# Retention tiles 16 to 35 in pairs: one order of TensorE's products for two tiles

## The chip, the cores and the metric

One core of a Trainium2 chip. The metric is the time of one execution on the device in microseconds (us). A kernel is run several times and the median stands for it.

## The reference

Two parts. Retention: for 8 batches and 8 heads, 576 positions of 64 features. Then a mixture of experts in which each of the 4,608 tokens goes to one of 8 experts.

```python
scores = scale * np.matmul(q, k.transpose(0, 1, 3, 2))
ret = scores * np.where(rel >= 0, gamma[:, None, None] ** rel, 0.0)
x = np.matmul(ret, v)                       # then (4608, 512)
logits = x @ w_gate                         # (4608, 8), the expert is argmax
gate_w = softmax(logits)[expert]; eom = sigmoid(x @ w_output_gate)
out[token] = gate_w * eom * (relu(x[token] @ w1[expert]) @ w2[expert])
```

## The kernel before

Everything is in float32. The 4,608 rows are 36 tiles of 128 tokens; nine tiles are two batches (576 + 576 rows), so in what follows c = g % 9 is the place of tile g in its pair of batches, and tile c = 4 holds the end of one batch and the start of the next. Causality over earlier tiles is carried by a running state, the sum of k times v per head: it is kept in PSUM (`st_ps`), copied to SBUF after each tile (`stT`), and started anew at c = 0 and c = 4. The decay is folded into q and v beforehand.

The order is written out by hand: every engine, and every DMA queue, runs its instructions in the order in which the code emits them, and waits on what it needs at the head of its queue. Lines 979 to 1053 are the loop over the tiles. For tile g, TensorE gets, in this order:

- `scores(g + 1)` (L767): 32 products in an array shape of 64 x 64, into two banks of PSUM of a ring of three; VectorE then multiplies both banks by the causal mask into `S_sb` (L771, two instructions);
- the state product of tile g (L800): 16 products, 64 x 64, into `o_ps`; none at c = 0;
- scores by v (L804): 16 products, 128 x 64, onto the same `o_ps`; ScalarE copies the result to `xT` (L807), VectorE turns it to rows `xq` (L812), and SyncE stores them in DRAM (L816);
- `update(g)` (L785): 16 products, 128 x 64, into `st_ps`, copied by ScalarE to `stT` (L788); none at c = 8;
- `k_rows(g + 1)` (L745): four transposes of k, 128 x 128, into the bank `kt`, copied by ScalarE to `kn` (L750, L752), which the next update reads; none for c = 8;
- once in four tiles, `logits` (L822): 32 products, 128 x 32, and two tiles later `ranks` (L860 to L867), six products of 128 x 128 in bfloat16, which read what VectorE has made of the logits (`gate_a`, eight instructions from L828 to L849). `gate_b`, `gate_d` and `gate_c` (L872 to L902, VectorE) and two exponentials (L854, L893, ScalarE) make from these the slots and weights that GpSimd scatters to the lists of the experts.

Beside these stand, in the queues of the other engines: GpSimd multiplies q by its decay (`prep_q`, L723), four tiles ahead. From tile 23 on, ScalarE multiplies all eight heads of v by theirs (`prep_va`, L739, eight instructions a tile, three tiles ahead; five heads for tiles 20 to 22, the others go to GpSimd at L730). SyncE loads q, k and v of tile g + 6 (L690) into the buffers that tile g gives up, each load behind the last product that reads that buffer. `PLAN` (L50) says after which tiles GpSimd sends a scatter to the lists (L906, "s") or gathers rows for the first expert (L257, "g"). The weights of the first expert are rounded on ScalarE (L231) and their rests taken on VectorE (L234, two halves, one behind a tile). Behind tile 35 the products of the first expert begin (L469, `mm1_columns`).

Of the kernel before, what the change touches and what calls it, by code (L numbers as in the profile page):

```python
# [10 lines left out]
F32 = mybir.dt.float32  # L11
F32R = mybir.dt.float32r
# [37 lines left out]
PLAN = {8: "ss", 12: "ss", 16: "ss", 20: "ss", 11: "", 15: "", 19: "", 22: "sg", 23: "g", 24: "gs", 25: "gs", 26: "s",  # L50
        27: "ss", 28: "ss", 29: "sg", 30: "gg", 31: "gs", 32: "gs", 33: "gg", 34: "gs", 35: "ss"}
LISTS = (20, 28, 31)
W1_AT = (4, 11, 17, 25)


@with_exitstack
def tile_retention_moe(
# [628 lines left out]
    st_ps, stcur = [None], [None]  # L686
# [54 lines left out]
    def k_rows(g):  # L741

        kt = ps_1.tile([P, 512], F32, name="kt")
        for p in range(NP):
            T.transpose(kt[:, P * p:P * p + P], pk[g, 1][:, P * p:P * p + P], ident)  # L745
# [8 lines left out]
    def scores(g):  # L754


        sc = [banks[(2 * g + r) % 3] for r in range(2)]
        S_sb = wk.tile([P, 2, NP, P], F32, name="S_sb")
        edge = g % CPB == 4
        for pp in (0, 2):  # L760
            for late in range(2):
                for p in (pp, pp + 1):
                    h = (late + p) % 2
                    i = slice(64, P) if late else slice(0, 64) if edge else slice(0, P)
                    for r in range(2):
                        s = slice(64 * r, 64 * r + 64)
                        T.matmul(sc[r][64 * h:64 * h + 64, p, i], lhsT=pk[g, 1][s, P * p + 64 * h:P * p + 64 * h + 64],  # L767
                                 rhs=qs[g][s, p, i], start=True, stop=True, skip_group_check=True)
        m = cmat_sb[:, 1 if edge else 0].rearrange("p (a b) i -> p a b i", a=1).broadcast_to([P, 2, 2, P])
        for r in range(2):  # L770
            V.tensor_tensor(out=S_sb[:, r].rearrange("p (a b) i -> p a b i", a=2),  # L771
                            in0=sc[r].rearrange("p (a b) i -> p a b i", a=2), in1=m, op=ALU.mult)
        return S_sb

    def update(g):
        c = g % CPB
        marks["u"] = marks["v"]
        if c == 8:
            return
        if c in (0, 4):  # L780
# [8 lines left out]
        stcur[0] = stT[g % 2]  # L789

    def out_x(g, S_sb, state):
        c = g % CPB
        o = o_ps[:, :, 256 * (g % 2):256 * (g % 2) + 256]
        part = lambda p, r: o[64 * ((p + r) % 2):64 * ((p + r) % 2) + 64, r, P * (p // 2):P * (p // 2) + P]
        order = [(p, (p + i) % 2) for p in range(NP) for i in range(2)]
        if state is not None:
            w = 64 if c == 4 else P
            for p, r in order:
                s = slice(64 * r, 64 * r + 64)
                marks["q"] = T.matmul(part(p, r)[:, 0:w], lhsT=state[s, p, :], rhs=qs[g][s, p, 0:w],  # L800
                                      start=(p < 2), stop=False, skip_group_check=True).ins
        marks.setdefault("q", last[0])
        for p, r in order:
            marks["v"] = T.matmul(part(p, r), lhsT=vs[g][:, 2 * p + r, :], rhs=S_sb[:, r, p, :],  # L804
                                  start=(state is None and p < 2), stop=True, skip_group_check=True).ins
        xT[g] = wk.tile([P, KB, P], F32, name="xT", bufs=5)
        A.copy(out=xT[g].rearrange("p (r s) i -> p r s i", r=2),  # L807
               in_=o[:, :, :].rearrange("p r (s i) -> p r s i", s=2))

    def x_rows(g):  # L810
        xq = xr[g] = wk.tile([P, 4, P], F32, name="xq", bufs=3)
# [3 lines left out]
    def store_x(g):  # L815
        SP.dma_start(out=xs[4 * P * g:4 * P * (g + 1)].rearrange("(p b) c -> p b c", b=4), in_=xr[g])  # L816
# [75 lines left out]
    def exp_b(n):  # L892
        A.activation(out=gt["zs"], in_=gt["zs"], func=AF.Exp, scale=-1.0)  # L893
# [82 lines left out]
        elif what == "s":  # L976
            todo.pop(0)(by=by)

    for g in range(NTILE):
        S_sb = S_next  # L980
        prev = stcur[0] if g % CPB != 0 else None
        n, late = divmod(g - GT, GT)
        if g == 0:
            for i in range(3):
                load(5, i)
        if g > 0:
            store_x(g - 1)
        if g < 4:
            load_rest(g)
        if g == 5:  # L990
            SP.dma_start(out=ents, in_=tokid)
        if g in W1_AT:
            wl.append(load_w(1, 0, W1_AT.index(g)))
        elif 30 <= g <= 32:
            wl.append(load_w(2, 0, g - 30))
        if g in LISTS:
            load_idx(0, LISTS.index(g), LISTS.index(g) + 1)
        if g == 4:
            V.tensor_copy(base2, base)
        if 0 < g < NTILE - 1:  # L1000
# [5 lines left out]
        while min(ready) < min(g + lead + 1, NTILE):  # L1006
# [6 lines left out]
        if g + 3 < NTILE:  # L1013
            prep_va(g + 3)
        if g in (8, 16, 20, 28):
            split_w(*wl.pop(0))
        elif n >= 0 and late == 1:
            gate_a(n)
        if sub:
            sub.pop()()  # L1020
        out_x(g, S_sb, prev)
        if g == NTILE - 1:
            last_x = transp_a(2)
# [9 lines left out]
        if g + 6 < NTILE:  # L1033
            for i, m in enumerate("qvu"):
                load(g + 6, i, marks[m])
        if g == 0:
            S_next = scores(1)
        if g < 2:
            more_gq(3 + g)
        if g + 1 < NTILE and (g + 1) % CPB != CPB - 1:  # L1040
            k_rows(g + 1)
        if g in (28, 32):
            sub.append(transp_a(g // 32))
        if n >= 0 and late == 0:
            gt["ps"] = ps_1.tile([P, 512], F32, name="lg_ps")
            logits(n, gt["ps"])
        elif n >= 0 and late == 2:
            exp_b(n)
            gate_d(n)
            if n >= 5:  # L1050
                gate_c(n)
        elif 0 <= n < 5 and late == 3:
            gate_c(n)
    last_x()
    psctx.close()
    pools["ps_h"] = mctx.enter_context(tc.tile_pool(name="ps_h", bufs=2, space=PSUM, side="right", reuse_waits="tile"))
# [536 lines left out]
```

## Time and profile before

| | |
|---|---|
| median of 3 runs | 544.37 us (543.6 to 544.88) |
| the profiled execution | 543.63 us |
| its span | 541.8 us |
| TensorE busy | 524.0 us (97%) |
| VectorE, ScalarE, GpSimd busy | 412.6, 296.1, 336.7 us |
| DMA | 102.98 MB, 190 GB/s mean over the span |

The span is the time between the first and the last instruction that the profiler recorded; the execution's own time is 1.8 us longer. Busy shares are averages over the retention (about the first 140 us) and the experts (the rest), in which different things wait. A matmul's end is modelled, so consecutive matmuls overlap in the rows; the distance from one start to the next is what one of them takes of TensorE. PE is TensorE, PEld its weight loads, DVE VectorE, ACT ScalarE, POOL GpSimd, SP SyncE; L767 is line 767 of the kernel before.

### The profile page before, as it was taken

What the parts mean: (1) busy time and instruction counts of PE and PEld (TensorE: products, weight loads), DVE (VectorE), ACT (ScalarE), POOL (GpSimd) and SP (SyncE); (2) the same over time, 40 slices, a digit from 0 to 9 for tenths busy, and PEclk for the clock granted to TensorE, in tenths of its full rate; (3) what the DMA queues carried; (4) which work ended last, traced back from release to release, by engine and by line L of the source; (5) the groups of instructions that cost most, each with busy time, mean ns of one, the idle gap of its engine ahead of it and who ended that gap; (6) DMA issues with size and microseconds to landing.
All of it is one profiled execution on the core that took longest, in us unless ns stands there. A gap on an engine that the chain in (4) does not pass through costs nothing.

```text
span 541.8 us, 14890 instructions
## 1 busy us (share of the span) xinstructions
PE 524.0 (97%) x5707; PEld 479.1 (88%) x5707; DVE 412.6 (76%) x772; ACT 296.1 (55%) x566; POOL 336.7 (62%) x354
## 2 busy tenths in 40 slices
PE   7999999999999999999999999999999999999994
PEld 4887888878897988998999999899999989999982
DVE  4678688987873759997798689869958976996650
ACT  5535579888343527645744664476355447635710
POOL 2859986887787777876655476456737555101821
PEclk9999999999999999999999999999999999999998
DMA  8999899879224424636643762565276356516511
GB/s 264 365 364 378 302 332 317 302 259 318 84 67 133 139 73 159 213 122 163 220 142 103 243 225 62 169 228 187 77 225 219 103 155 225 171 39 201 172 46 36
DMA packets 60444, 102.98 MB, mean 190 GB/s; under 512 B 11492, under 2 KB 23269, under 8 KB 60372
## 3 DMA queue, kind: packets, MB, share of 16 engines
q1 hardware_dynamic: 50628, 81.65, 45.7%
q0 software_dynamic: 9312, 19.71, 11.9%
q8 instruction: 45, 0.74, 0.5%
q10 hardware_dynamic: 432, 0.66, 0.4%
q14 instruction: 27, 0.22, 0.1%
HBM read 78.26 MB, written 23.86 MB: 188 GB/s over the span
## 4 chain that ended last, share of the span: by engine, by line
PE 50%; issue 16%; DVE 11%; DMA 8%; POOL 7%; ACT 5%; SPq 1%; POOLq 0%; DVEq 0%; ACTq 0%
PE h_ps L528 6%; PE o_ps L804 5%; PE y_ps L578 5%; POOL x_q L257 5%; PE sc L767 4%; PE y_ps L609 4%; PE y_ps L528 3%; PE h_ps L578 3%; DMA out_dram<-y,idx 3%; DMA st<-in_w_dram 3%; PE h_ps L609 3%; PE o_ps L800 2%; PE y_ps L450 2%; PE kt L745 2%; PE h_ps L389 2%
## 5 line engine op out<-in xcount | busy, mean ns | idle before, releaser
L257 POOL DMA_INDIRECT x_q<-xs,gidx x139 | 162.0, 1166 | 60.6 <-issue 35.4
L543 POOL DMA_INDIRECT out_dram<-y,idx x13 | 15.2, 1170 | 67.2 <-ACT y L588 62.3
L771 DVE TENSOR_TENSOR S_sb<-sc,cmat_sb 128x512 f32<-128x512 f32 x72 | 45.7, 676 | 8.2 <-PE sc L767 8.1
L578 PE MATMUL y_ps<-w2l,hh 128*128 128x512 f32 (+1 forms) x128 | 49.9, 390 | 0.0
L578 PE MATMUL y_ps<-w2h,hh 128*128 128x512 f32 (+1 forms) x128 | 49.9, 390 | 0.0
L723 POOL TENSOR_TENSOR q<-q,gq_sb 128x512 f32<-128x512 f32 x33 | 42.3, 1283 | 10.2 <-DMA q<-in_pack_dram 6.5
L212 DVE TENSOR_TENSOR w<-st,w 128x1024 fp32r<-128x1024 f32 x21 | 25.6, 1221 | 27.6 <-ACT w L202 27.6
L906 POOL DMA_INDIRECT lst<-ents,sli x36 | 38.7, 1074 | 10.2 <-issue 5.0
L578 PE MATMUL y_ps<-w2h,hl 128*128 128x512 f32 (+1 forms) x128 | 43.6, 390 | 0.0
L528 PE MATMUL h_ps<-t,w 128*128 128x300 f32 (+4 forms) x288 | 40.7, 293 | 0.0
L804 PE MATMUL o_ps<-S_sb,v 128*64 128x128 f32 x576 | 40.0, 279 | 0.4 <-POOL v L730 0.3
L181 DVE TENSOR_TENSOR st<-st 128x512 f32<-128x512 f32 x56 | 37.2, 685 | 3.7 <-DMA st<-in_w_dram 3.0
L219 ACT CAST w2h<-st 128x1024 fp32r<-128x1024 f32 x28 | 29.3, 1046 | 18.8 <-DMA st<-in_w_dram 18.8
L543 POOL DMA_INDIRECT out_dram<-yr,idx x21 | 21.1, 1005 | 29.2 <-ACT yr L641 11.9
L528 PEld LDWEIGHTS h_ps<-t,w 128*128 128x128 f32 x288 | 38.7, 188 | 0.2 <-DVE p L511 0.2
L807 ACT COPY xT<-o_ps 128x512 f32<-128x512 f32 x36 | 21.0, 582 | 31.0 <-PE o_ps L804 30.6
L804 PEld LDWEIGHTS o_ps<-S_sb,v 128*64 128x64 f32 x576 | 31.0, 136 | 6.2 <-issue 3.4
L767 PEld LDWEIGHTS sc<-q,k 64*64 64x64 f32 x1152 | 27.5, 133 | 9.9 <-issue 6.6
L812 DVE STREAM_TRANSPOSE xq<-xT 128x512 f32<-128x512 f32 x36 | 25.4, 706 | 14.2 <-ACT xT L807 11.7
L767 PE MATMUL sc<-q,k 64*64 64x64 f32 (+1 forms) x1152 | 33.9, 248 | 2.1 <-DVE S_sb L771 1.0
L739 ACT ACTIVATE v<-v,gkf 128x64 f32<-128x64 f32 x137 | 35.0, 340 | 0.0
L223 DVE TENSOR_TENSOR w2l<-st,w2h 128x1024 fp32r<-128x1024 f32 x28 | 34.1, 1217 | 0.3
(247 smaller groups left out, 1466.2 us busy)
## 6 DMA issues: line engine op xcount, KB each, us to landing
st<-in_w_dram SPq DMA_DIRECT2D x36, 512.0 KB
st<-in_w_dram SPq DMA_DIRECT2D x56, 256.0 KB
k<-in_pack_dram SPq DMA_DIRECT2D x36, 256.0 KB
xs<-xq SPq DMA_DIRECT2D x36, 256.0 KB
q<-in_pack_dram SPq DMA_DIRECT2D x35, 256.0 KB
v<-in_pack_dram SPq DMA_DIRECT2D x35, 256.0 KB
yr<-yg SPq DMA_DIRECT2D x12, 256.0 KB
x_q<-xs,gidx POOLq DMA_INDIRECT x139
```

The lines of the kernel that those rows point to most:

```text
L181: V.tensor_tensor(out=RAW[e, q, name], in0=RAW[e, q, a], in1=RAW[e, q, b], op=op)
L257: i = G.indirect_dma_start(out=XG[e, t][:, u, :], out_offset=None, in_=seen, in_offset=bass.IndirectOffsetOnAxis(ap=gidx[:, e, 4 * t + u:4 ...
L528: last[0] = T.matmul(ps[:, b], lhsT=x[:, k, P * b:P * b + P], rhs=y[:, k], start=(j < 2 and i == 0), stop=(i == 5), skip_group_check=True).ins
L543: i = G.indirect_dma_start(out=out, out_offset=bass.IndirectOffsetOnAxis(ap=rows, axis=0), in_=y, in_offset=None, bounds_check=NT - 1, oob ...
L578: last[0] = T.matmul(ps, lhsT=a, rhs=b, start=(j == 0), stop=(j == 3 * FB - 1)).ins
L609: last[0] = T.matmul(ps[:, 0:n], lhsT=a, rhs=b, start=(j == 0), stop=(j == 3 * FB - 1)).ins
L723: (V if g < 3 else G).tensor_tensor(out=qs[g], in0=qs[g], in1=gq_sb[:, :, c0:c0 + P], op=ALU.mult)
L739: A.activation(out=v[:, h], in_=v[:, h], func=AF.Copy, scale=gk_sb[:, g % CPB, h])
L767: T.matmul(sc[r][64 * h:64 * h + 64, p, i], lhsT=pk[g, 1][s, P * p + 64 * h:P * p + 64 * h + 64], rhs=qs[g][s, p, i], start=True, stop=Tru ...
L771: V.tensor_tensor(out=S_sb[:, r].rearrange("p (a b) i -> p a b i", a=2), in0=sc[r].rearrange("p (a b) i -> p a b i", a=2), in1=m, op=ALU.mult)
L804: marks["v"] = T.matmul(part(p, r), lhsT=vs[g][:, 2 * p + r, :], rhs=S_sb[:, r, p, :], start=(state is None and p < 2), stop=True, skip_gr ...
L906: i = G.indirect_dma_start(out=lst, out_offset=bass.IndirectOffsetOnAxis(ap=sli[:, t, :], axis=0), in_=ent[:, t], in_offset=None)
```

## The change

The loop over the tiles ends at tile 15. `out_x` is taken apart into `q_state`, `s_v` and `x_copy`, `k_rows` and `scores` are told which banks to use, and a new loop takes two tiles a step. Four banks (the ring of three and `kt`) are used as two sets of two. The masked scores of every third tile go into memory of a later buffer (`hl2`), so that three of them can live at once. q is prepared three tiles ahead, v on ScalarE up to tile a + 2 and then b + 2.

```diff
+SOLO = 16
...
-    for g in range(NTILE):
+    for g in range(SOLO):
...
+    S, ready_va = {SOLO: S_next}, [SOLO + 3]
+    quads = [*banks, ps_1.tile([P, 512], F32, name="kt").rearrange("p (a b) -> p a b", a=NP)]
+    quad_of = lambda a, i: quads[2 * ((a // 2 + i) % 2):2 * ((a // 2 + i) % 2) + 2]
...
+    store_x(SOLO - 1)
+    ahead(SOLO)
+    split_w(*wl.pop(0))
+    update(SOLO)
+    indirect("s", marks["u"])
+    more(SOLO + 6, 1, "u")
+    rows_of((SOLO + 1, SOLO + 2), quads[2:4])
+    indirect("s", marks["t"])
+    lows.pop(0)()
+    count(SOLO // GT - 1)
+
+    for a in range(SOLO + 1, NTILE, 2):
+        o, b = a - 1, a + 1
+        n, odd = divmod(a - GT - 1, GT)
+        on = b < NTILE
+        pa, pb = (PLAN.get(g, "s") + ".." for g in (a, b))
+        if a > SOLO + 1:
+            store_x(o - 2)
+            store_x(o - 1)
+        weights(a)
+        ahead(a)
+        if not odd:
+            gate_a(n)
+        S[a] = scores(a, quad_of(a, 0))
+        if not odd:
+            exp_a(n)
+        indirect(pa[0], marks["s"])
+        more(a + 6, 1, "s")
+        fresh = True
+        for g in (o, a):
+            if g % CPB:
+                q_state(g, states[g - 1], fresh)
+                fresh = False
+            more(g + 6, 0, "q")
+        if on:
+            weights(b)
+            ahead(b)
+            S[b] = scores(b, quad_of(a, 1))
+            more(b + 6, 1, "s")
+        indirect(pa[1], marks["s"])
+        if not odd:
+            ranks(n)
+            gate_b(n)
+            gate_d(n)
+        elif sub:
+            sub.pop()()
+        if on:
+            update(a)
+        if not odd:
+            exp_b(n)
+            gate_c(n)
+        for g in (o, a):
+            s_v(g, S.pop(g), False)
+            more(g + 6, 2, "v")
+            if g == o:
+                indirect(pb[0] if on else ".", marks["v"])
+        for g in (o, a):
+            x_copy(g)
+        if b in (20, 28):
+            split_w(*wl.pop(0))
+        if on:
+            update(b)
+            indirect(pb[1], marks["u"])
+        if odd:
+            for i in range(2):
+                if lows:
+                    lows.pop(0)()
+        if not on:
+            last_x = transp_a(2)
+        for g in (o, a):
+            x_rows(g)
+        rows_of((a + 2, b + 2), quad_of(a, 0))
+        if a in (27, 31):
+            sub.append(transp_a(a // 31))
+        if odd and on:
+            count(n + 1)
```

`ahead(g)` is `prep_q` up to tile g + 3, `prep_v` and `prep_va` up to g + 2; `weights(g)` loads weights and lists at the tiles where they were loaded before; `more(g, i, m)` loads q, k or v (i = 0, 1, 2) of tile g behind the products marked m; `rows_of` is `k_rows` for the tiles that need it; `count(n)` is `logits(n)`.

## Rows read from the trace of the kernel before

**Rows 1.** A stretch of four tiles: us, then busy PE, PEld, DVE, ACT, POOL, clock, DMA, GB/s.

```profile
86.25:100.99 14.74, 14.40 (x376) 12.54 (x375) 12.69 (x32) 14.22 (x51) 13.33 (x16) 1.00 0.97 314
```

**Rows 2.** Timeline of PE, one tile: start us, us, what.

```profile
65.73 0.90 PE L767 MATMUL sc<-q,k 64*64 64x128 f32 x32
66.45 0.62 PE L800 MATMUL o_ps<-q,stT 64*64 64x128 f32 x16
67.00 1.09 PE L804 MATMUL o_ps<-S_sb,v 128*64 128x128 f32 x16
67.92 0.63 PE L785 MATMUL st_ps<-v,kn 128*64 128x64 f32 x16
68.49 0.66 PE L745 MATMUL kt<-ident,k 128*128 128x128 f32 x4
69.07 0.90 PE L767 MATMUL sc<-q,k 64*64 64x128 f32 x32
```

**Rows 3.** Timeline of PE, windows of some 0.05 us across two changes of shape.

```profile
66.78 0.29 PE L800 MATMUL o_ps<-q,stT 64*64 64x128 f32 x4
67.00 0.33 PE L804 MATMUL o_ps<-S_sb,v 128*64 128x128 f32 x2
...
68.27 0.29 PE L785 MATMUL st_ps<-v,kn 128*64 128x64 f32 x4
68.49 0.33 PE L745 MATMUL kt<-ident,k 128*128 128x128 f32 x1
```

**Rows 4.** Timeline of PEld, the same tile; idle time before a group in brackets.

```profile
65.73 0.76 PEld L767 LDWEIGHTS sc<-q,k 64*64 64x64 f32 x32 [0.17 <-issue]
66.39 0.43 PEld L800 LDWEIGHTS o_ps<-q,stT 64*64 64x64 f32 x16
67.00 0.85 PEld L804 LDWEIGHTS o_ps<-S_sb,v 128*64 128x64 f32 x16 [0.17 <-issue]
```

**Rows 5.** Timeline of PE, tiles 24 to 30: idle before a group in brackets.

```profile
100.99 1.08 PE L822 MATMUL lg_ps<-xT,wg_sb 128*32 128x128 f32 x32 [0.34 <-DVE zs L900]
...
111.84 1.01 PE L767 MATMUL sc<-q,k 64*64 64x128 f32 x30 [0.27 <-DVE S_sb L771]
...
121.28 0.67 PE L800 MATMUL o_ps<-q,stT 64*64 64x128 f32 x16 [0.34 <-ACT stT L788]
```

**Rows 6.** Timeline of ACT: one tile of eight heads, a weight's rounding, an exponential.

```profile
97.02 0.56 ACT L807 COPY xT<-o_ps 128x512 f32<-128x512 f32 x1
97.48 0.37 ACT L788 COPY stT<-st_ps 128x256 f32<-128x256 f32 x1
97.75 0.58 ACT L752 COPY kn<-kt 128x512 f32<-128x512 f32 x1
98.23 2.03 ACT L739 ACTIVATE v<-v,gkf 128x64 f32<-128x64 f32 x8
...
114.45 1.04 ACT L231 CAST w<-st 128x1024 fp32r<-128x1024 f32 x1
...
139.98 0.20 ACT L893 ACTIVATE zs<-zs 128x4 f32<-128x4 f32 x1 [1.18 <-DVE zs L874]
```

**Rows 7.** Timeline of DVE: gate_a from first to last of eight, masks, a weight's rest.

```profile
89.42 0.32 DVE L828 STREAM_TRANSPOSE lg_ps<-lg_ps 128x128 f32<-128x128 f32 x1
...
91.14 0.23 DVE L849 TENSOR_REDUCE oh<-oh 128x8 bf16<-128x40 bf16 x1
...
95.84 1.28 DVE L771 TENSOR_TENSOR S_sb<-sc,cmat_sb 128x512 f32<-128x512 f32 x2
...
98.25 2.18 DVE L234 TENSOR_TENSOR w<-st,w 128x512 fp32r<-128x512 f32 x1
```

**Rows 8.** Timelines of SP and POOL: loads of tile 22, and the wait for its q.

```profile
74.27 0.33 SPq L690 DMA_DIRECT2D q<-in_pack_dram  x1
...
75.66 0.39 SPq L690 DMA_DIRECT2D v<-in_pack_dram  x1
...
80.46 1.27 POOL L723 TENSOR_TENSOR q<-q,gq_sb 128x512 f32<-128x512 f32 x1 [0.85 <-DMA q<-in_pack_dram]
```

More of the change, by code (lines that the diff above doesn't have):

```diff
@@ L739, in prep_va, with k_rows @@
             A.activation(out=v[:, h], in_=v[:, h], func=AF.Copy, scale=gk_sb[:, g % CPB, h])
-    def k_rows(g):
-        kt = ps_1.tile([P, 512], F32, name="kt")
+    def k_rows(g, kt=None):
+        if kt is None:
+            kt = ps_1.tile([P, 512], F32, name="kt")
         for p in range(NP):
-            T.transpose(kt[:, P * p:P * p + P], pk[g, 1][:, P * p:P * p + P], ident)
+            marks["t"] = T.transpose(kt[:, P * p:P * p + P], pk[g, 1][:, P * p:P * p + P], ident).ins
         kn[g] = wk.tile([P, 512], F32, name="kn")
@@ L752, in k_rows, with scores @@
             A.copy(out=kn[g], in_=kt)
-    def scores(g):
-        sc = [banks[(2 * g + r) % 3] for r in range(2)]
-        S_sb = wk.tile([P, 2, NP, P], F32, name="S_sb")
+    def scores(g, sc=None):
+        sc = sc or [banks[(2 * g + r) % 3] for r in range(2)]
+        if g > SOLO and g % 3 == 0:
+            S_sb = hpa.tile([P, 2, CW], F32R, name="hl2").bitcast(F32).rearrange("p a n -> p (a n)")[:, 0:8 * P]
+            S_sb = S_sb.rearrange("p (r a i) -> p r a i", r=2, a=NP)
+        else:
+            S_sb = wk.tile([P, 2, NP, P], F32, name="S_sb")
         edge = g % CPB == 4
@@ L766, in scores @@
                         s = slice(64 * r, 64 * r + 64)
-                        T.matmul(sc[r][64 * h:64 * h + 64, p, i], lhsT=pk[g, 1][s, P * p + 64 * h:P * p + 64 * h + 64],
-                                 rhs=qs[g][s, p, i], start=True, stop=True, skip_group_check=True)
+                        marks["s"] = T.matmul(sc[r][64 * h:64 * h + 64, p, i],
+                                              lhsT=pk[g, 1][s, P * p + 64 * h:P * p + 64 * h + 64],
+                                              rhs=qs[g][s, p, i], start=True, stop=True, skip_group_check=True).ins
         m = cmat_sb[:, 1 if edge else 0].rearrange("p (a b) i -> p a b i", a=1).broadcast_to([P, 2, 2, P])
@@ L788, in update, with q_state, s_v, x_copy @@
         A.copy(out=stT[g % 2], in_=st_ps[0])
[L789 to L805, printed above, removed]
+        stcur[0] = states[g] = stT[g % 2]
+    o_of = lambda g: o_ps[:, :, 256 * (g % 2):256 * (g % 2) + 256]
+    part = lambda g, p, r: o_of(g)[64 * ((p + r) % 2):64 * ((p + r) % 2) + 64, r, P * (p // 2):P * (p // 2) + P]
+    both = [(p, (p + i) % 2) for p in range(NP) for i in range(2)]
+    def q_state(g, state, fresh=True):
+        w = 64 if g % CPB == 4 else P
+        for p, r in both:
+            s = slice(64 * r, 64 * r + 64)
+            marks["q"] = T.matmul(part(g, p, r)[:, 0:w], lhsT=state[s, p, :], rhs=qs[g][s, p, 0:w],
+                                  start=(fresh and p < 2), stop=False, skip_group_check=True).ins
+    def s_v(g, S_sb, fresh):
+        for p, r in both:
+            marks["v"] = T.matmul(part(g, p, r), lhsT=vs[g][:, 2 * p + r, :], rhs=S_sb[:, r, p, :],
+                                  start=(fresh and p < 2), stop=True, skip_group_check=True).ins
+    def x_copy(g):
         xT[g] = wk.tile([P, KB, P], F32, name="xT", bufs=5)
         A.copy(out=xT[g].rearrange("p (r s) i -> p r s i", r=2),
-               in_=o[:, :, :].rearrange("p r (s i) -> p r s i", s=2))
+               in_=o_of(g).rearrange("p r (s i) -> p r s i", s=2))
+    def out_x(g, S_sb, state):
+        if state is not None:
+            q_state(g, state)
+        marks.setdefault("q", last[0])
+        s_v(g, S_sb, state is None)
+        x_copy(g)
     def x_rows(g):
@@ L1005, in tile_retention_moe @@
         plan = PLAN.get(g, "s" if g > 8 else "") + ".."
-        while min(ready) < min(g + lead + 1, NTILE):
+        while min(ready) < g + lead + 1:
             if ready[0] <= ready[1]:
@@ L1032, in tile_retention_moe @@
         indirect(plan[1], marks["u"])
-        if g + 6 < NTILE:
-            for i, m in enumerate("qvu"):
-                load(g + 6, i, marks[m])
+        for i, m in enumerate("qvu"):
+            load(g + 6, i, marks[m])
         if g == 0:
@@ L1039, in tile_retention_moe @@
             more_gq(3 + g)
-        if g + 1 < NTILE and (g + 1) % CPB != CPB - 1:
+        if (g + 1) % CPB != CPB - 1:
             k_rows(g + 1)
-        if g in (28, 32):
-            sub.append(transp_a(g // 32))
         if n >= 0 and late == 0:
@@ L1049, in tile_retention_moe, with ahead @@
             gate_d(n)
-            if n >= 5:
-                gate_c(n)
-        elif 0 <= n < 5 and late == 3:
+        elif n >= 0 and late == 3:
             gate_c(n)
+    S, ready_va = {SOLO: S_next}, [SOLO + 3]
+    quads = [*banks, ps_1.tile([P, 512], F32, name="kt").rearrange("p (a b) -> p a b", a=NP)]
+    quad_of = lambda a, i: quads[2 * ((a // 2 + i) % 2):2 * ((a // 2 + i) % 2) + 2]
+    def ahead(g):
+        for i, f, lead in ((0, prep_q, 3), (1, prep_v, 2)):
+            while ready[i] < min(g + lead + 1, NTILE):
+                f(ready[i])
+                ready[i] += 1
+        while ready_va[0] < min(g + 3, NTILE):
+            prep_va(ready_va[0])
+            ready_va[0] += 1
@@ new lines, in weights, with more, rows_of @@
+    def weights(g):
+        if g in W1_AT:
+            wl.append(load_w(1, 0, W1_AT.index(g)))
+        elif 30 <= g <= 32:
+            wl.append(load_w(2, 0, g - 30))
+        if g in LISTS:
+            load_idx(0, LISTS.index(g), LISTS.index(g) + 1)
+    def more(g, i, m):
+        if g < NTILE:
+            load(g, i, marks[m])
+    def rows_of(tiles, sets):
+        for g, ps in zip(tiles, sets):
+            if g < NTILE and g % CPB != CPB - 1:
+                k_rows(g, ps.rearrange("p a b -> p (a b)"))
@@ new lines, in count @@
+    def count(n):
+        gt["ps"] = ps_1.tile([P, 512], F32, name="lg_ps")
+        logits(n, gt["ps"])
+    store_x(SOLO - 1)
[54 more added lines that the diff above has]
+        for g in (o, a):
+            x_copy(g)
+        if b in (20, 28):
[16 more added lines that the diff above has]
+            count(n + 1)
@@ L1054, in tile_retention_moe @@
+    store_x(NTILE - 2)
     last_x()
```

17 lines of the change are left out of this document (4 added, 13 removed).

## The prediction

> **What bounds the kernel now.** I began with the table of busy shares over the span: TensorE is busy for 97% of it. Then the same by stretches of four tiles in the part that is changed, because a mean over the span hides what else is full there. It shows TensorE busy for 14.40 of 14.74 us, but ScalarE for 14.22, GpSimd for 13.33 and VectorE for 12.69 [rows 1]. TensorE sets the pace, and three others have little room. The reader should keep both halves of that in mind.
>
> Next the timeline of TensorE over one tile [rows 2]. From start to start the groups take 0.72 (scores), 0.55 (state product), 0.92 (scores by v), 0.57 (update) and 0.58 us (transposed k): 3.34 us a tile. Each includes what passes before the next group begins, and that differs. Look at the weight loads of the same tile: before the scores (64 x 64 behind 128 x 128) and before the scores by v (128 x 64 behind 64 x 64) the queue idles for 0.17 us; before the state product, which has the shape of the scores, it idles not at all [rows 4]. So there is a price on a change of the array's shape, and none on a new group.
>
> Two close views size it [rows 3]. The last four state products start at 66.78; three steps lead there from 66.45 [rows 2], 0.11 each, so the next was due at 66.89. The scores by v begin at 67.00, 0.11 late, and their first product takes 0.33 where later ones take 0.27 to 0.29: some 0.05 more. At the other change the last four update products start at 68.27; two steps of 0.06 make 68.39, the transposes begin at 68.49 and the first again takes 0.33. I take 0.155 us a change (0.10 to 0.11, and 0.05).
>
> **The change, part by part.** *What it removes: changes of shape.* Before, tiles 16 to 35 have three each (into the scores, into the scores by v, out of the update), 60. Logits behind transposes add one at tiles 20, 24, 28 and 32; tile 26 has no k to transpose, so its scores follow an update directly, one less: 63. After, scores and state products of two tiles share one run of 64 x 64, updates and scores by v one of 128 x 64, transposes one of 128 x 128: ten pairs of three, 30. The tail of tile 16 (update, k, logits) adds 3. Four logits behind transposes add 4. The ranks now stand between the second scores and the update, where before they stood beside transposes of their own shape: one more in five pairs, 5. The pair of tiles 34 and 35 begins straight from an update, one less: 41. Saved: 22 times 0.155, **3.4 us**. All of it lies on TensorE, which is the bound.
>
> *The products themselves* are the same in number and size, so nothing for them. The scatters and gathers of GpSimd keep their order and number; the masks' third buffer is other memory, no added instruction. Costed at nothing: GpSimd is busy for 13.33 of 14.74 us [rows 1] and prepares q three tiles ahead, so it can fall a pair behind (some 6 us) before the scores wait for it.
>
> *Old waits in this stretch.* TensorE waits 0.34 us for VectorE before the logits, 0.27 for the masks and 0.34 for ScalarE's state copy [rows 5], 0.95 in all. In the pair the logits come a whole pair after `gate_c`, the masks have a second set of banks, and the first state copy has two state products and a scores group ahead of its use. I take all 0.95 out; the bounds are 0 and 0.95.
>
> *New wait 1: the state's bank.* `update(b)` writes the PSUM bank that ScalarE's copy behind `update(a)` reads, and only two scores by v (1.84 us) lie between. On ScalarE that copy stands behind the preparation of v for two tiles, 16 instructions: 2 x 2.03 = 4.06 us [rows 6]. In a pair with ranks VectorE does `gate_a` (1.95 us) and four masks (2 x 1.28) before it can give the sums that the exponential reads [rows 7]: about 5.0 us into the pair. Behind the exponential ScalarE has two output copies (0.46 each), a state copy (0.27) and two k copies (0.48 each) [rows 6], to 7.3 us. That pair takes TensorE 2 x 3.34 - 0.46 + 0.32 for ranks and their change = 6.5 us, so ScalarE enters the next one 0.8 us late, ends with v at 4.9 and with the state copy at 5.2. TensorE wants the bank at 0.72 + 0.44 + 0.44 + 0.67 + 0.16 + 0.46 + 1.84 = 4.7 us. It stands 0.5 us, in the three pairs (23, 27, 31) that have both 16 preparations and no logits ahead: 1.5 us. Behind the waiting update are the transposes, the logits and the whole next pair. Bounds 0 (ScalarE enters on time) and 3 x 1.5 (it enters 1 us later).
>
> *New wait 2: VectorE into the ranks.* Without ranks a pair gives VectorE two masks, two halves of a weight's rest and two row transposes: 2.56 + up to 4.36 [rows 7] + 1.4 = 8.3 us, where TensorE takes 6.2 + 1.2 for logits. `gate_a` then begins up to 0.9 late; the ranks have 0.4 us of room. At most two pairs (19, 27): I take 0.2 each, 0.4 (0 to 1).
>
> *DMA.* Six loads and two stores now come in a bunch in each pair. The loads of v of tiles 22, 24, ... are issued behind `s_v(o)`, 4.2 us into one pair, and wanted on ScalarE about 2.7 us into the next: 5.2 us later. Before, it was three tiles less the way to the end of the scores by v, 3 x 3.34 - 2.2 = 7.8 us. The one landing that the trace shows is that of tile 22's q: issued at 74.27, waited for until 80.46, 6.2 us, with a weight of 512 KB ahead of it; its v was issued at 75.66 and nobody waited [rows 8]. I take 0 for this, because without the weight ahead a landing is some 1.7 us shorter (an estimate: 512 KB at the 314 GB/s of [rows 1]), and keep 1 us in each of six pairs as the upper end, which is the third rival.
>
> *The sum.* -3.4 - 0.95 + 1.5 + 0.4 = -2.45 us. Against the profiled execution's own 543.63 that is 541.2; the median of the runs is 0.74 above that execution, so against 544.37 I forecast **541.9 us**. What follows tile 35 is TensorE's work again, and shifts with it.
>
> **The rivals.** *ScalarE is the bound (543.4 us).* By rows, four tiles cost it 4 x (0.46 + 0.27 + 0.48 + 2.03) = 13.0, an exponential's wait of 1.18, some 0.3 for two exponentials [rows 6], together 14.4, and 1.04 more where a weight is rounded; it was 14.22 busy in 14.74 [rows 1]. TensorE would want 13.6. If that wait stays in each four, tiles 21 to 32 gain nothing: of the 22 changes only those of the other eight tiles count, some 9 x 0.155 less 0.4, about 1.0 us. For it: ScalarE has 0.5 us free in four tiles. Against it: 1.2 of the 14.4 is a wait that grows shorter when the gates stand early in the pair, and after tile 32 it has no v. The Trainium skill, page TensorEngine Tiling (Array Packing), section PSUM Bottleneck, says that shaping the array speeds up TensorE but not the copying out of PSUM, which may then become the limit; by that rule this rival, and 543.4, would be the forecast. The trace agrees only in part: ScalarE is within 4% of full there, but more than half of its time is v, which isn't PSUM.
>
> *More than forecast (540.2 us):* neither new wait appears, -4.35. For it: each rests on VectorE and ScalarE being late by half a microsecond. Against: four engines near full rarely fit without a seam.
>
> *Slower (547 us): v lands late.* Place: ScalarE's queue, in the pairs 19 to 29. Its preparation of v stands ahead of the state copy; when v isn't there, that copy, the output copies and the k copies all wait. Price: landings of 6.2 us, as for tile 22's q, against a lead of 5.2 make 1.0 us in each of six pairs, 6 us, less the 1 us that the forecast's own waits share: 541.9 + 5 = 547. It decides from a landing of some 5.8 us on; at 5.2 it costs nothing. For it: DMA was busy for 0.97 of the stretch [rows 1], and it must now bring the same bytes in less time. Against: tile 22's q had a weight ahead of it, and only one pair in this stretch has one.
>
> *That the pause isn't saved* (each group pays whatever stands before it) would give 544.4 plus the new waits; the missing pause before the state product [rows 4] speaks against it, and I put it with the last rival.
>
> **How the numbers follow.** About 0.2%, 1.1 us, is what a measurement of this kernel can tell from no change. The forecast has a chance of 0.50 (541 to 543), more than forecast 0.12, ScalarE the bound 0.23 (542.4 to 544.6, some of it faster by more than 1.1 us, most within), slower 0.15. Faster therefore 0.70, same 0.15, slower 0.15. The range reaches from the end of the second case, 540.0, through the old waits staying and the upper ends of new waits 1 and 2 in part, to 544.8, and leaves out the late v and a little at the low end. The likeliest case alone has 541 to 543.
>
> **What would show it right or wrong.** Right: in the timeline of weight loads, pauses of 0.17 us at three places in a pair, four with ranks; pairs of about 6.5 and 7.4 us from scores to scores; the first product of the experts at about 138 us instead of 140.5. The state copy as the releaser of an update in three odd pairs shows new wait 1. The first rival shows as ScalarE without idle time from tile 20 to tile 32 and many updates and scores waiting for its copies. The third shows as ScalarE's L739 waiting for a transfer of v. The forecast is wrong if the pauses go and the stretch doesn't shrink: then a wait has taken their place, and its releaser names it. It is wrong at its root if a run of one shape over two tiles still shows the pauses.

## The result, and the profile after

| | before | after |
|---|---|---|
| median of 20 runs each, side by side | 544.77 us | 549.24 us |
| ratio, 95% interval | | 1.0078 [1.0052, 1.0105] |
| profiled execution (its span) | 543.63 (541.8) | 549.78 (547.9) |
| from the transposed k of tile 16 to the first expert product | 71.98 | 78.30 |
| after that to the end of the span | 401.3 | 402.4 |

The kernel became slower by 4.5 us in the medians, where 541.9 us was forecast. Here and below a ratio counts the undisturbed runs alone and a median all of them, so that a ratio can be smaller than that of the medians beside it. The forecast's range, 540.0 to 544.8, doesn't hold it. In the profiled executions the difference is 6.15 us, and the stretch in which the tiles go in pairs is 6.3 us longer: the first expert product comes at 145.49 us, not at about 138. What lies ahead of the stretch is 1.3 us shorter, what lies behind it 1.1 longer. The first product of the experts in the kernel before, then the two ends of the stretch in the changed kernel:

```profile
140.47 1.70 PE L469 MATMUL h_ps<-xc,w 128*128 128x256 f32 x12
...
67.19 0.65 PE L747 MATMUL kt<-ident,k 128*128 128x128 f32 x4
...
145.49 1.69 PE L470 MATMUL h_ps<-xc,w 128*128 128x256 f32 x12
```

A pair is one step of the new loop and is named by its `a`: pair 19 begins with the scores of tile 19. First the timeline of TensorE of the changed kernel, at the tail of tile 16 and in the first pair (line numbers are the changed kernel's: update L791, transposes L747, logits L837, scores L772, state products L805, scores by v L810, ranks L875).

```profile
68.58 0.69 PE L791 MATMUL st_ps<-v,kn 128*64 128x64 f32 x16 [0.73 <-ACT kn L754]
...
70.79 0.90 PE L772 MATMUL sc<-q,k 64*64 64x128 f32 x32
...
75.75 1.09 PE L747 MATMUL sc<-ident,k 128*128 128x128 f32 x8
76.77 0.32 PE L772 MATMUL sc<-q,k 64*64 64x128 f32 x1
```

This is the pair as it was meant: 5.98 us from scores to scores (70.79 to 76.77), with no update for tile 17 in it. The pauses at a change of shape are still there, but few. The timeline of weight loads of the same pair:

```profile
70.79 0.76 PEld L772 LDWEIGHTS sc<-q,k 64*64 64x64 f32 x32 [0.20 <-issue]
71.45 0.87 PEld L805 LDWEIGHTS o_ps<-q,stT 64*64 64x64 f32 x32
...
76.77 0.13 PEld L772 LDWEIGHTS sc<-q,k 64*64 64x64 f32 x1 [0.17 <-POOL tick L920]
```

0.17 to 0.20 us where the scores begin, nothing before the 32 state products of two tiles: a run of one shape has no pause, as [rows 4] had it.

Now what took its place. The waits of TensorE from 64 to 150 us (us in total, times, longest):

```profile
PE st_ps L791 <- ACT stT L794: 6.4, 5, 2.8
PE lg_ps L875 <- DVE oh L859: 2.2, 2, 1.3
PE kt L772 <- issue: 1.1, 1, 1.1
PE st_ps L791 <- ACT kn L754: 0.7, 1, 0.7
```

10.5 us of idle time, where the kernel before had 2.12 in its stretch. The line with "issue" is idle time for which the profile has no releaser, that is, no other engine or transfer that ended it; of the 2.12 before, 0.89 was of this kind. The five waits of the update for ScalarE's copy of the state are not alike. The timeline of TensorE has four of them here, and the products behind the longest, and a wait of the ranks:

```profile
87.00 0.18 PE L875 MATMUL lg_ps<-oh,cbf_sb 128*128 128x32 bf16 x1 [0.97 <-DVE oh L859]
...
91.71 0.69 PE L791 MATMUL st_ps<-v,kn 128*64 128x64 f32 x16 [1.92 <-ACT stT L794]
92.33 1.09 PE L747 MATMUL sc<-ident,k 128*128 128x128 f32 x8
...
98.28 0.69 PE L791 MATMUL st_ps<-v,kn 128*64 128x64 f32 x16 [0.32 <-ACT stT L794]
...
113.70 0.69 PE L791 MATMUL st_ps<-v,kn 128*64 128x64 f32 x16 [2.77 <-ACT stT L794]
114.32 0.88 PE L747 MATMUL sc<-ident,k 128*128 128x128 f32 x4
114.99 1.06 PE L747 MATMUL kt<-ident,k 128*128 128x128 f32 x4
115.98 1.94 PE L837 MATMUL lg_ps<-xT,wg_sb 128*32 128x128 f32 x32
...
121.62 0.18 PE L875 MATMUL lg_ps<-oh,cbf_sb 128*128 128x32 bf16 x1 [1.27 <-DVE oh L859]
...
131.70 0.69 PE L791 MATMUL st_ps<-v,kn 128*64 128x64 f32 x16 [0.77 <-ACT stT L794]
```

ScalarE's timeline says why two of them are long. The state copy (L794) stands behind v (L740), and v waited for its transfer:

```profile
89.39 2.02 ACT L740 ACTIVATE v<-v,gkf 128x64 f32<-128x64 f32 x8 [2.45 <-DMA v<-in_pack_dram]
91.31 0.35 ACT L794 COPY stT<-st_ps 128x256 f32<-128x256 f32 x1
...
111.38 2.02 ACT L740 ACTIVATE v<-v,gkf 128x64 f32<-128x64 f32 x8 [1.85 <-DMA v<-in_pack_dram]
113.30 0.35 ACT L794 COPY stT<-st_ps 128x256 f32<-128x256 f32 x1
...
114.51 1.05 ACT L232 CAST w<-st 128x1024 fp32r<-128x1024 f32 x1
...
120.02 0.62 ACT L302 CAST xc<-w2h 128x512 fp32r<-128x512 f32 x1 [3.22 <-DVE w2h L298]
```

The first wait of TensorE, 1.92 us, is shorter than the 2.45 us by which v was late. The second, 2.77 us, is longer than 1.85: without the late v some 0.9 us of it would have stayed (an estimate, 2.77 less 1.85).

The transfers, in the timeline of SP's queue:

```profile
79.72 2.28 SPq L691 DMA_DIRECT2D q<-in_pack_dram  x2
82.30 0.66 SPq L657 DMA_DIRECT2D ls<-lst  x1
83.06 0.41 SPq L691 DMA_DIRECT2D k<-in_pack_dram  x1
83.58 0.85 SPq L691 DMA_DIRECT2D v<-in_pack_dram  x2
...
100.45 0.46 SPq L153 DMA_DIRECT2D st<-in_w_dram  x1
...
104.73 1.20 SPq L691 DMA_DIRECT2D v<-in_pack_dram  x2
```

The first v was issued at 83.58, 6.8 us into its pair, since SP issues in order and the second load of q, a load of the list and one of k stood ahead of it; ScalarE wanted it at 89.39 - 2.45 = 86.94, 3.4 us later, and it landed after 5.7. The second was issued 4.2 us into its pair, as reckoned, with a weight of 512 KB ahead; ScalarE wanted it at 109.53, 4.8 us later, and it landed after about 6.6.

The second late v goes on to VectorE. Its timeline, at the rounding of a weight (L235), the first operation of `gate_a` (L843), and what the ranks wait for (L859):

```profile
83.46 0.69 DVE L235 TENSOR_TENSOR w<-st,w 128x512 fp32r<-128x512 f32 x1 [1.58 <-ACT w L232]
85.30 0.29 DVE L843 STREAM_TRANSPOSE lg_ps<-lg_ps 128x128 f32<-128x128 f32 x1
...
115.59 2.58 DVE L235 TENSOR_TENSOR w<-st,w 128x512 fp32r<-128x512 f32 x2 [4.70 <-ACT w L232]
...
119.91 0.28 DVE L843 STREAM_TRANSPOSE lg_ps<-lg_ps 128x128 f32<-128x128 f32 x1
121.37 0.19 DVE L859 TENSOR_TENSOR oh<-lg_ps,m 128x32 bf16<-128x32 f32 x1
```

ScalarE's part of the rounding stands behind the late v and the state copy, VectorE waits 4.70 us for it with `gate_a` behind, and `gate_a` begins 2.0 us after the logits have ended (115.98 + 1.94 to 119.91). That is the wait of 1.27 us of the ranks at 121.62. The first wait of the ranks, 0.97 us at 87.00, has no late v ahead of it: VectorE waited 1.58 us for ScalarE's part of the rounding until 83.46, and `gate_a` began 1.4 us after its logits had ended (82.78 + 1.08 to 85.30), but the first late v was wanted only at 86.94.

Last the clock, in busy times by stretches (the stretch, its us, then PE, PEld, DVE, ACT, POOL, granted clock, DMA share, GB/s):

```profile
92.30:99.40 7.10, 6.78 (x176) 6.12 (x172) 6.22 (x9) 7.01 (x24) 6.42 (x7) 1.00 0.90 309
114.30:118.00 3.70, 3.70 (x48) 2.88 (x48) 2.41 (x2) 2.50 (x5) 2.54 (x5) 0.54 0.54 160
```

Behind 1.92 us of idle time the granted clock stayed at 1.00; behind 2.77 it was 0.54, which is the level of 1.2 GHz with a part of the stretch at 2.4. The logits there took 1.94 in place of 1.08, the two tiles' transposes 1.66 (114.32 to 115.98) in place of 1.02 (92.33 to 93.35): 1.5 us in all.

All this is read from one execution of the changed kernel; the 20 runs lie between 545.52 and 553.6 us, and whether each of them had the same waits isn't known.

### The profile page after: what moved, and what is told of

Read it like the earlier page. It is cut to its first block, busy times and chain, and to the rows that moved or that the text cites. A ratio compares the mean times of both kernels' runs of the same rounds, so it can differ in the third digit from the quotient of the medians.

```text
span 547.9 us, 14925 instructions
## 1 busy us (share of the span) xinstructions
PE 521.8 (95%) x5707; PEld 480.7 (88%) x5707; DVE 414.6 (76%) x772; ACT 295.5 (54%) x566; POOL 337.1 (62%) x354
## 4 chain that ended last, share of the span: by engine, by line
PE 59%; issue 12%; DVE 8%; POOL 8%; ACT 5%; DMA 5%; SPq 2%; POOLq 0%; ACTq 0%; DVEq 0%
PE h_ps L529 11%; PE y_ps L579 7%; PE y_ps L529 6%; PE y_ps L610 6%; PE h_ps L610 6%; PE o_ps L810 4%; PE sc L772 4%; POOL x_q L258 3%; ACT v L740 2%; PE st_ps L791 2%; PE y_ps L451 2%; PE o_ps L805 2%; PE kt L747 2%; PE h_ps L579 2%; POOL lst L1286 2%
## 5 line engine op out<-in xcount | busy, mean ns | idle before, releaser
L777 DVE TENSOR_TENSOR S_sb<-sc,cmat_sb 128x512 f32<-128x512 f32 x53 | 33.9, 677 | 9.0 <-PE sc L772 7.4
L544 POOL DMA_INDIRECT out_dram<-yr,idx x21 | 21.9, 1041 | 29.5 <-ACT yr L642 12.5
L740 ACT ACTIVATE v<-v,gkf 128x64 f32<-128x64 f32 x137 | 34.9, 342 | 4.3 <-DMA v<-in_pack_dram 4.3
L772 PE MATMUL sc<-q,k 64*64 64x128 f32 (+1 forms) x992 | 32.5, 247 | 1.5 <-issue 1.5
L772 PEld LDWEIGHTS sc<-q,k 64*64 64x64 f32 x992 | 27.8, 134 | 6.9 <-issue 6.1
L810 PE MATMUL o_ps<-S_sb,v 128*64 128x128 f32 x480 | 32.7, 277 | 0.5 <-POOL v L731 0.3
L529 PE MATMUL y_ps<-t,wx 128*128 128x300 f32 (+4 forms) x216 | 31.4, 294 | 0.5 <-DVE p L512 0.5
L529 PEld LDWEIGHTS y_ps<-t,wx 128*128 128x128 f32 x216 | 29.6, 188 | 1.3 <-DVE p L512 0.8
```

The source lines that it names most:

```text
L529: last[0] = T.matmul(ps[:, b], lhsT=x[:, k, P * b:P * b + P], rhs=y[:, k], start=(j < 2 and i == 0), stop=(i == 5), skip_group_check=True).ins
L544: i = G.indirect_dma_start(out=out, out_offset=bass.IndirectOffsetOnAxis(ap=rows, axis=0), in_=y, in_offset=None, bounds_check=NT - 1, oob ...
L772: marks["s"] = T.matmul(sc[r][64 * h:64 * h + 64, p, i], lhsT=pk[g, 1][s, P * p + 64 * h:P * p + 64 * h + 64], rhs=qs[g][s, p, i], start=T ...
L810: marks["v"] = T.matmul(part(g, p, r), lhsT=vs[g][:, 2 * p + r, :], rhs=S_sb[:, r, p, :], start=(fresh and p < 2), stop=True, skip_group_c ...
```

## The experiments

Theory: the smaller number of shape changes gave what was forecast, and a chain ate it: v lands late, ScalarE's state copy and rounding stand behind it, TensorE and VectorE behind those. Rivals: ScalarE or VectorE is simply full; or the order itself costs TensorE something. **The later runs were made under other conditions than the two kernels of the first section:** on all the chips that they ran on, the kernel before itself took 566 to 571 us and not 544. Whether that lies in the chips or in something else at the time isn't known; the expectations speak of a second kind of chip. So each run is compared with the kernel before beside it, and waits are read apart from totals. Line numbers of edits with a new buffer for v are 3 higher.

**v two tiles earlier** (with two more buffers):

```
-            more(g + 6, 2, "v")
+            more(g + 8, 2, "v")
```

> The changed kernel, with two more buffers for v, so that each v is loaded two tiles earlier. Theory (v lands later than ScalarE wants it, and ScalarE's queue holds the state copy behind it): ScalarE's two waits for v (2.45 and 1.85 us) go, with them the two long waits of TensorE for the state copy (1.92 and 2.77 us) and the stretch at the lower clock that follows the longer one (some 1.5 us): about 5 us less than the changed kernel, 544 us. Rival (ScalarE's queue is full, v on time or not): the waits for the state copy stay, under 1.5 us less than the changed kernel, 548 us or more.

572.88 beside 567.71, ratio 1.013 [1.0053, 1.0206]. No wait of ScalarE for v is left, and the waits for the state copy are 0.2 us, but the time, expected 5 us under the changed kernel's, did not fall below the kernel before.

**Half of the preparation of v behind `update(a)`**:

```
+        ahead_va(a)
...
         if on:
             update(a)
+            ahead_va(b)
```

> The changed kernel, with the preparation of v for the second tile of a pair moved on ScalarE from ahead of the first state copy to behind it. Theory of the late v: the state copy no longer waits for the v that is late (it is the second tile's), and v has some 1.5 us more to land; TensorE's waits for the state copy, 6.4 us in all, fall under 1.5 us; 543 to 545 us. Rival (a full ScalarE): the same work in the queue, the wait moves to the output copies, 547 us or more.

575.01 beside the same, 1.0167 [1.0095, 1.0238]. No wait for the state copy is there either, and ScalarE waits for no v; but the ranks wait 1.6 and 0.6 us for VectorE, so their wait needs no late v:

```profile
PE lg_ps L875 <- DVE oh L859: 1.6, 1, 1.6
```

**VectorE's rests ahead of the rounding**:

```
+        if odd:
+            for i in range(2):
+                if lows:
+                    lows.pop(0)()
         if b in (20, 28):
             split_w(*wl.pop(0))
...
-        if odd:
-            for i in range(2):
-                if lows:
-                    lows.pop(0)()
```

> The changed kernel, with VectorE's halves of a weight's rest placed ahead of that weight's rounding in the same pair (so they work on the weight rounded before, or come a pair later). Theory: VectorE no longer waits for the rounding (6.3 us in the two pairs with one), gate_a is on time behind it and TensorE's waits for the ranks (0.97 and 1.27 us) go; the late v stays: 547 us. Rival (VectorE's waiting only follows from ScalarE's, which was held by v): no change beyond 0.5 us, 549 us.

571.43, 1.0033 [0.9963, 1.0104], which could be no change. Two of the waits of TensorE (64 to 155 us):

```profile
PE st_ps L791 <- ACT stT L794: 3.1, 2, 2.8
PE o_ps L805 <- issue: 2.2, 8, 0.4
...
```

No wait of the ranks is in the whole list, while a late v is there. On ScalarE's timeline it is the eight heads of the same pair, 2.43 us late where the first profile had 2.45:

```profile
93.15 2.02 ACT L740 ACTIVATE v<-v,gkf 128x64 f32<-128x64 f32 x8 [2.43 <-DMA v<-in_pack_dram]
```

So the two are separate costs: here the late v with its state copy came without a wait of the ranks, in the run before the ranks' wait without a late v.

**All three.**

> The three edits together. If each takes away its own wait, what is left is the saving of 22 changes of shape, 3.4 us, less small waits: 541 to 543 us, faster than the kernel before. If ScalarE is full whatever its order, 545 us or more.

570.85, 1.0106 [1.0019, 1.0193].

In this profile no wait that the theory names is left, and the gain had not come. Next the two kernels unedited under the later conditions, and the edits without the buffers.

> The kernel before, unedited, for its profile on the chip on which the others of this group run: TensorE's idle time put down to issue is 0.9 us from the logits of tile 16 to the first product of the experts in the profile shown. If issue is a matter of the chip, it is as long here as in the edited kernels on the same chip; if the pairs bring it, it stays under 1 us here.

> The changed kernel, unedited, on the same chip as the others of this group: 1.005 to 1.011 of the kernel before, with waits of TensorE for the state copy and for the ranks of 6 to 9 us together.

> The two reorderings together (half of v's preparation behind the first state copy; the rests ahead of the rounding), no buffer added. Theory of the late v: no wait of TensorE for the state copy over 0.5 us, none for the ranks; 4 to 7 us less than the changed kernel, at or below the kernel before (0.993 to 1.002). Rival (the pairs cost something else, instruction supply or a full ScalarE): the waits are gone and the time stays above 1.004 of the kernel before.

> All three edits, again, beside a profile of the kernel before on the same chip. Theory: 0.990 to 1.000 of the kernel before. Rival (something else): above 1.004, with TensorE's idle time in the stretch put down to issue and longer than in the kernel before.

Kernel before: 566.46 (one execution, median of the 29 runs beside 567.7). Changed kernel: 572.95, 1.0076 [1.0038, 1.0115], the same ratio as at first, with other waits. The 6 to 9 us of waits for the state copy and the ranks that were expected are not in its profile: ScalarE waits for no transfer of v, the ranks not for VectorE, and what TensorE waits for other engines is this (66 to 160 us):

```profile
PE st_ps L791 <- ACT kn L754: 0.7, 1, 0.7
PE st_ps L791 <- ACT stT L794: 0.6, 1, 0.6
...
PE st_ps L791 <- ACT v L740: 0.5, 1, 0.5
```

So under the later conditions the kernel lost its 0.8% without the waits of the first profile, and that a wait is absent from an edited run doesn't show that the edit took it away.

Second and third edit: 572.66, 1.0091 [1.0049, 1.0133]. All three: 571.72, 1.0044 [1.0003, 1.0084]. TensorE's waits in the kernel before, from 66 to 152 us:

```profile
PE sc L767 <- issue: 2.4, 8, 0.4
PE o_ps L800 <- issue: 1.4, 4, 0.5
PE o_ps L804 <- issue: 1.1, 4, 0.3
...
```

and in the one with all three edits (e6_again), from 66 to 155:

```profile
PE o_ps L808 <- issue: 2.6, 9, 0.4
PE sc L775 <- issue: 1.5, 5, 0.4
...
```

Idle time with no releaser ("issue") is 4.9 us in the stretch before, 6.2 after, where the two profiles of the first section had 0.89 and 1.13. Two places in the timeline of TensorE of the unedited changed kernel show what kind it is: it falls in the middle of a run of scores, behind others of the same run.

```profile
101.00 0.93 PE L772 MATMUL sc<-q,k 64*64 64x128 f32 x20
102.28 0.45 PE L772 MATMUL sc<-q,k 64*64 64x128 f32 x8 [0.35 <-issue]
...
104.74 0.25 PE L772 MATMUL sc<-q,k 64*64 64x64 f32 x1 [0.45 <-issue]
```

Idle time counts these pauses too low, because a product's modelled end covers part of each. Counted from the start of the product ahead of a pause to the start of the one behind it, they take 9.0 and 7.8 us of the stretch in the two profiles of the kernel before (80.23 and 80.25 us) and 11.8 and 12.5 in the two of the unedited changed kernel (82.50 and 82.26). The waits that have a releaser, counted in the same way, take 1.2 and 1.7 us, and 2.7 and 1.5. What is left is 70.1 and 70.8 us before, 68.1 and 68.3 in pairs: 2 to 2.5 us are still saved here, and the longer pauses take 2.7 to 4.7.

**ScalarE's part of the decay of v left out of both kernels.** These two leave out the scaling of v by ScalarE, so tokens go to other experts and the expert part is longer; they are compared with each other alone. A second run of the second and third edit, and a second profile of the kernel before (570.35 us), ran beside them.

```
-        for h in range(heads(g)):
+        for h in range(0):
```

> The kernel before, with the multiplication of v by its decay on ScalarE left out (three to eight heads of tiles 14 to 35 keep v as it was loaded, so tokens go to other experts and the part behind tile 35 may take another time). It is the base for the next run; from the transposes of tile 16's k to the first product of the experts it should take what the kernel before takes on the same chip, within 1 us, because TensorE and not ScalarE sets its pace.

> The changed kernel with the same multiplication left out, so that ScalarE waits for no v and has half its work. Theory (the late v and what queues behind it ate the saving): the stretch from the transposes of tile 16's k to the first product of the experts is 2.5 to 4.5 us shorter than in the previous run, the whole about 0.995 of it. Rival (the pairs cost TensorE's instruction supply what they save in changes of shape): the stretch is within 1 us of the previous run or longer, with more idle time put down to issue.

> The two reorderings again (half of v's preparation behind the first state copy; the rests ahead of the rounding), for a second profile and interval: 1.005 to 1.013 of the kernel before if this is the chip of the last two groups, 0.993 to 1.000 if it is one with as little idle time put down to issue as in the profile shown first.

636.68 and 645.54, 1.4% apart in the medians. With no v on ScalarE at all, the pairs are still slower: their stretch is 81.55 us against 79.78, idle time with no releaser in it 6.88 against 4.30 (12.1 against 8.0 from start to start), and no wait for the state copy remains. That speaks against ScalarE as the bound, and under these conditions against late v as the whole. Without the pauses and the waits that have a releaser 67.6 us are left against 70.7: the pairs save 3.1 us here, and the pauses take 4.2. Only 1.8 of the 10.2 us between the two spans lie in the stretch; 6.8 lie behind it, where both run the same code. e4_second: 575.55, 1.0097 [1.0058, 1.0137].

**The first update, and fewer pairs.** The transposes of tile 18 ahead of the update of tile 16, with all three edits (e7), and pairs from tile 28 on only, four instead of ten (f), with the second and third edit and what the longer first loop then has to load, round and finish itself:

```
+    rows_of((SOLO + 2,), quads[3:4])
     update(SOLO)
...
-    rows_of((SOLO + 1, SOLO + 2), quads[2:4])
```

```
-SOLO = 16
+SOLO = 28
```

> The changed kernel unedited, on whatever chip this is. Where the kernel before takes about 544 us: 549 again (ratio 1.008), with waits of TensorE for the state copy of several us and a late v. Where it takes about 568 us: 572 again, with 5 to 7 us of issue in the stretch from the transposes of k of tile 16 to the first expert product.

> All three edits together (v two tiles earlier, half of ScalarE's v preparation behind the update of the first tile, VectorE's rests ahead of the rounding), and the transposes of k of tile 18 ahead of the update of tile 16, so that the copy of k of tile 16 has time. Theory (late v, rests, and first update ate a saving of 3.4 us): on a chip where the kernel before takes about 544 us, 541 (ratio 0.994). On one where it takes about 568: no wait for ScalarE of 0.73 us any more, 0.7 us less than the 571.3 of the run without this edit. Rival (pairs cost the supply of instructions what the shape changes save): 0.2 to 1 per cent slower than the kernel before, on the second kind of chip with 5 us or more of issue in the stretch, against 4.3 to 4.9 in the kernel before.

> Pairs from tile 28 on alone (4 pairs in place of 10), with the half of the v preparation moved and the rests ahead of the rounding. If the loss of the pair order on the second kind of chip goes with the number of pairs, it is 0.4 of that of the ten pairs: ratio 1.003 to 1.004. If it is a cost of the first pairs alone (loads of v at tiles 20 to 26, the first update), nothing or a gain: 0.997 to 1.000.

> The same two edits with all ten pairs, beside the run with four. Theory on a chip where the kernel before takes about 544 us: 542 to 544. On one where it takes about 568: 572 to 573 as in the two runs of it so far, ratio 1.009.

> Pairs from tile 28 on alone, as the run before this one, which left out the load of the second list of the expert at tile 28 (its gathers took other rows); with that load in. If the loss on this kind of chip goes with the number of pairs: 1.003 to 1.004 where ten pairs give 1.004 to 1.009. If four pairs lose as much as ten (1.006 or more), the loss is not a cost for each pair.

> The kernel with all three edits and the earlier transposes again, beside the one with four pairs. On a chip where the kernel before takes 567 to 571 us: 1.003 to 1.008 as before, 6 to 7 us of issue in the stretch. On a chip where the kernel before takes about 544: theory 541, rival 544 or more.

Changed kernel again: 574.73, 1.0159 [1.008, 1.0237]. e7: 573.82, 1.0064 [1.0011, 1.0118], and 574.51, 1.0093 [1.0042, 1.0144]; the wait of the first update fell from 0.73 to 0.29 us, the time showed nothing of it. Ten pairs with two edits: 571.5, 1.0039 [0.9979, 1.0098]. Four pairs: 573.04, 1.0028 [0.9978, 1.0078]. Where the load of the second list was left out as well, 571.13, 1.0079 [1.0042, 1.0115]. These intervals overlap, so whether the loss goes with the number of pairs stays open: the runs could not tell it.

What follows from all of it. In the first profile the releasers name v's transfer and VectorE's order, and the second and third edit show that these are two costs and not one. That the edits take the waits away is not shown, because the unedited kernel had hardly any of them under the later conditions; nor is it shown that the pairs would win by 3 us where the kernel before takes 544. Under the later conditions pauses with no releaser grow by more than the pairs save, in each of the three profiles of pairs without an edit of the order beside that of the order before; their cause is open. There nine profiles of ten pairs with the whole computation and an edit have 80.7 to 84.5 us from the transposes of tile 16 to the first expert product, the unedited changed kernel 82.3 and 82.5, the kernel before 80.2 and 80.3. Behind the stretch, where the code is the same, they lie between 413.0 and 418.9 us, so how much of a loss in the whole belongs to the pairs can't be read from one profile each. No version was measured faster than the kernel before.

## Why the prediction was wrong, step by step

**Right: the mechanism and its size.** Without waits the stretch went from 69.86 to 67.79 us, 2.1 less, although 1.5 was lost to the clock: 3.6, where 22 changes at 0.155 made 3.4. The number of changes was right too: TensorE's products in the stretch change their shape 63 times in the trace before and 41 times in the one after. That the array's shape has a price and a new group has none holds [rows 3, 4]. The undisturbed pairs took 5.98 (without an update, 0.57 less than 6.5) and, from 76.77 to 83.80, 7.03 (without a state product for tile 18, 0.44 less than 7.4), as forecast. The old waits of [rows 5] went: no masks, no logits, and the state copies that remain are the new kind.

**The step that failed: the term DMA, taken as 0.** The sum had nothing for it; in the first profile TensorE waited 4.7 us behind two late v's, of which some 0.9 would have stayed without them. The place and the mechanism stood in the rival "v lands late", with a chance of 0.15. Two things were wrong in the term. The lead of 5.2 us was counted from the products that set the transfer free, not from SP's own queue: in pair 19 the load of the list, a q and a k stand ahead, the issue came 2.6 us later, and 3.4 us of lead were left. And a landing "without the weight ahead" was thought shorter by 1.7 us than the 6.2 of [rows 8]; the first had no weight ahead and took 5.7, the second had one and took 6.6. Nor was tile 22's q the one landing that the trace before shows; GpSimd waited for tile 23's too, issued at 77.98 with no weight ahead and there at 83.0, after 5.0 us and not 4.5:

```profile
83.04 1.27 POOL L723 TENSOR_TENSOR q<-q,gq_sb 128x512 f32<-128x512 f32 x1 [1.30 <-DMA q<-in_pack_dram]
```

The upper end, 1 us in each of six pairs, was near in sum and wrong in shape: 1.92 and 2.77 us in two pairs, 4.7 in all, none in the others.

**New wait 1** was sound apart from that. In pairs 23 and 31 the update waited 0.32 and 0.77 us, forecast 0.5; that of pair 27 is part of the 2.77 us put down to its late v. In pair 29 it waited 0.64, which was not forecast: ScalarE had stood still for 3.22 us, to 120.02, until VectorE, behind the rounding, had turned the gathered rows that its cast at L302 reads.

**New wait 2** named the two pairs, behind the logits of tiles 19 and 27, and had the sum of work on VectorE, but not its order: 0.97 and 1.27 us against 0.2 each. The rounding is divided between two engines, and VectorE's half at the head of its queue waits for ScalarE's with the gate behind it. I used the sum of the work on VectorE, where the head of its queue decides.

**Not foreseen at all:** the update of tile 16 right behind its own k copy, 0.73 us (before, scores and more lay between), and the clock, 1.5 us.

The sum with the measured terms: -3.6 (shapes), -1.23 (old waits in the stretch, 0.62 for ScalarE among them), +1.73 (new wait 1 in three pairs), +4.69 (late v), +2.24 (ranks), +1.5 (clock), +0.73 (first update), +0.24 (no releaser) = 6.3 us, the 6.32 of the stretch. The 3.6 is what is left when the other terms are taken out, so that the sum closes is no evidence of its own; forecast were -3.4, -0.95, +1.5 and +0.4.

**The rivals.** ScalarE as the bound is wrong as put: it stood idle, waiting for v, 4.3 us in the stretch. The slower rival was right in sign and, for the largest single term, in cause: two late v's and not six. That its 547 is only 2 us under the measured 549.24 is in part luck, since 1.5 us of clock, most of 2.24 us of ranks and 0.73 us of the first update were not in it; the clock and the second wait of the ranks came behind the second late v, the others did not. *More than forecast* was put at 540.2; its own -4.35 from 544.37 makes 540.0.

## What to carry to other kernels

Count a transfer's lead from where it stands in its issuing queue, behind every load and wait ahead of it, and price its landing by the longest in the same busy stretch. When steps of several tiles are put together to save TensorE work, the time between an operand's buffer coming free and its next use shrinks for all other engines; each in-order queue then has to be read from its head, not summed. A saving of 0.6% on an engine that is 97% busy needs its neighbours' slack checked first: in the first profile TensorE waited 4.7 us behind two transfers that were 2.45 and 1.85 us late, where the shapes had saved 3.6.

## What the runs showed of the hardware that was not expected

Behind an idle time of 2.77 us the granted clock was 0.54 from 114.30 to 118.00, while behind one of 1.92 us it stayed at 1.00. The run with VectorE's rests first had 2.79 us of idle time and 0.55 behind it (95.48 to 99.00). And under the later conditions the same unedited kernel took 566 to 571 us with idle times of 0.2 to 0.5 us, many in the midst of TensorE's runs of short products, for which the profile has no releaser. They sum to 4.3 to 4.9 us of the stretch in the order before (three profiles) and 5.2 to 7.0 in ten pairs. That it is the supply of instructions is a guess that no run shows: TensorE's pauses grew while the larger instruction queue moved the same 45 packets, 0.74 MB, in every run, at 0.5 to 0.6% of the transfer engines' time.
